# A pre-norm block with sliding-window attention and a gated feed-forward part: maxima of two query tiles turned in one pass, projection weights due sooner, second layer norms and the last gate and up products issued sooner

## The chip, the cores and the metric

The kernel runs on one core of a Trainium2 chip. The core has five engines with a queue of instructions each: TensorE (PE) multiplies matrices and transposes, VectorE (DVE) and ScalarE (ACT) work on rows and read PE's results, GpSimd (POOL) works here on rows in SBUF, and SyncE (SP) issues the transfers (DMA). The queues run beside each other and meet at semaphores. PE writes into PSUM, which the kernel uses as eight banks of 128 x 512 floats; a bank is in use from the first product written to it until the last read of it. The metric is the device time of one execution in microseconds, the median of several; lower is better.

## The reference

```python
h  = x + A(layernorm(x))          # S = 2048 tokens, D = 448
h2 = h + B(layernorm(h))

def A(x):                         # 16 heads of 28, window of 256 keys
    q, k, v = split(x @ wqkv)
    scores = q @ k.T * 28 ** -0.5
    scores = where(0 <= i - j < 256, scores, -1e9)
    return (softmax(scores) @ v) @ wo

def B(x):                         # 1792 hidden columns
    return (gelu(x @ w_gate) * (x @ w_up)) @ w_down
```

All in float32. The kernel keeps that precision by writing an operand as the sum of two rounded numbers, a "hi" part (ACT rounds it, L308) and a "lo" part, the rest (DVE or POOL subtract, L311), and by multiplying hi x hi, hi x lo and lo x hi.

## The kernel before

Nothing here is a loop of the hardware. The program is recorded as a list of operations, each with an engine, a cost, a latency, a due number called key and what it reads and writes; `Lists.run` then plays them against a model of the engines and writes each engine's queue in the order that comes out (L110 to L203): at each step, among the operations of an engine that could start soonest, the one with the lowest key goes next. A transfer is reckoned to land after a fixed time and its share of a common bus. PSUM banks are handed out by `allowed`: score products use banks 0 and 1, probability products and the passes of the maxima 2 and 3 (bank 7 joins both once all projections are done), the layer norms, v, projections and output products 6 and 7, and attention sums 4 and 5. The order is thus fixed when the program is built; on the chip the queues only wait for each other.

The tokens are 16 tiles of 128, in four chunks (c) of four tiles. The heads are four groups (g) of four, worked on in two passes (p) over the sequence. So attention has 16 blocks, B = 8p + 2c + g % 2, and a block's keys begin at 16 B.

*Before a block.* `layer_norms` computes mean and variance (DVE L338, L340; POOL L329 to L335), normalises (ACT L352), transposes on PE (L357) and writes the transposed tile xT as hi and lo. `values` multiplies v (PE L468), `project_tile` q and k (PE L502); q and k go to DRAM and return in another layout as rq and rk (SP L512, L514, L534). The weights are loaded into the staging tile raw (wqk at SP L476, two halves of 512 columns in turn; wv at L452, columns 0 to 895) and split by ACT and DVE. The second pass over the sequence needs new weights: its wv and wqk go through the same raw, wv first, and each is split into the place of the first pass's weights once these have had their last use.

*In a block.* `scores(B, i, j)` multiplies query tile i of head j with its three key tiles (PE L551, 84 rows) and takes the row maximum (DVE L555) into column j of mx. `maxima(B, i)` negates four such columns, splits them into hi and lo (DVE L570, L573) as eight columns of mhl, turns them into eight rows by one PE product against the identity (L582, 72 columns of weights, 128 columns moved), and ACT copies these eight rows into rows 96 to 103 of rq for all four heads (ACT L308, `rq<-bank`). `probs(B, m, j)` then multiplies key tile m with up to three query tiles on 104 rows (PE L622), so that the maximum is subtracted within the product, and ACT takes the exponential (L626). Key tile m meets query tiles max(0, m-2) to min(3, m). POOL cuts the diagonal blocks (L637), `attend` multiplies with v (PE L656), `drain` divides by the sums, and `output` multiplies with wo (PE L694) and adds to the residual hres (DVE L697).

*Feed-forward.* The 1792 hidden columns are 14 records of 128 (gate, up and down weights). Four groups of 4, 4, 3 and 3 records run over the four chunks, which makes 56 calls of `product`: 11 gate and 11 up products (PE L783), gelu (ACT L801), multiplication (DVE L803), rounding to hi (ACT L308) and lo (DVE L311), and 12 down products (PE L810) into four banks, which are added to hres after the last record of a group (DVE L815) and, in the last group, stored (SP L818). The keys of product n begin at 1000 + 30 n (FFN). The first two products are "early": they run in attention's last blocks and their results wait in the front part of v's tile (ACT L789). `weights` loads a record (SP L735) into raw, or into one of two parts of v's tile, and splits it; its tile is chosen by the line with q.

Second layer norms are those of h ahead of the feed-forward part. Tiles 0 to 3 run in the second pass's blocks. Tiles 4 to 15 have keys FFN + 30 t - 60; chunk c's first product has FFN + 120 c.

Of the kernel before, what the change touches and what calls it, by code (L numbers as in the profile page):

```python
# [8 lines left out]
F32 = mybir.dt.float32  # L9
# [9 lines left out]
NF = F // 128  # L19
# [19 lines left out]
FFN = 1000  # L39
EARLY = 2  # L40
# [26 lines left out]
class Lists:  # L67
# [42 lines left out]
    def run(self, allowed, idle):  # L110
# [49 lines left out]
        while n:  # L160
# [25 lines left out]
            o.fin = t + lat  # L186
# [20 lines left out]
def block_kernel(ctx: ExitStack, tc, x, wqk_in, wv_in, wo_in, ffn_in, out):  # L207
# [32 lines left out]
    mx = [pool.tile([128, 4], F32, name=f"mx{i}") for i in range(4)]  # L240
# [214 lines left out]
    def wv_split(p):  # L455
        key = 80 if p else -38
        for b in range(0, 4, 2):
            op("act", 0.47, 0.57, key, lambda b=b: to_hi(wv[:, 0, b:b + 2], wv_raw[p][:, b:b + 2]),
               [WVRAW(p, b, 2)], [WV(0, b, 2)])
            op("dve", 0.54, 0.63, key + 1, lambda b=b: to_lo(wv[:, 1, b:b + 2], wv_raw[p][:, b:b + 2], wv[:, 0, b:b + 2]),  # L460
               [WVRAW(p, b, 2), WV(0, b, 2)], [WV(1, b, 2)], port=True)
# [16 lines left out]
    def wqk_split(m):  # L478
        i = m % 4
        key = -34 + 3 * m if m < 4 else 16 * 8 - EDGE - WIN - 10 + m  # L480
        op("act", 0.53, 0.64, key, lambda: to_hi(wqk[i][:, 0], wqk_raw[m % 2]), [WQKRAW(m % 2)], [WQK(i, 0)])
        op("dve", 0.6, 0.7, key, lambda: to_lo(wqk[i][:, 1], wqk_raw[m % 2], wqk[i][:, 0]),
           [WQKRAW(m % 2), WQK(i, 0)], [WQK(i, 1)], port=True)
# [59 lines left out]
    def scores(B, i, j):  # L543
# [10 lines left out]
        def most():  # L554
            nc.vector.tensor_tensor_reduce(junk[s % 2][:, o:384], bank[b.k][:, o:384], mask[:, o:384],  # L555
                                           1.0, -BIG, OP.add, OP.max, mx[i][:, j:j + 1])
# [7 lines left out]
    def maxima(B, i):  # L564
        u, k = B % 2, (4 * B + i) % 3
        a, m = mx[i], mhl[k]
        key = 16 * B + 4 * i + LAG_T

        def hi():
            nc.vector.tensor_scalar(m[:, 0:4], a, -1.0, None, op0=OP.mult)  # L570

        def lo():
            nc.vector.scalar_tensor_tensor(m[:, 4:8], a, -1.0, f(m[:, 0:4]), op0=OP.mult, op1=OP.subtract)  # L573
        al = [("mx", i, j) for j in range(4)]
        op("dve", 0.08, 0.175, key - 2.5, hi, al, [("mh", k)], port=True)
        op("dve", 0.08, 0.17, key - 2.5, lo, al + [("mh", k)], [("ml", k)], port=True)
        b = Bank("extra")

        def tr():
            nc.tensor.matmul(bank[b.k][0:72, 384:512], m[:, 0:72], one_r,  # L582
                             start=True, stop=True)
# [142 lines left out]
    def weights(i, key):  # L726

        q = 0 if i < 2 else i % 3
# [42 lines left out]
    def product(n, i, c, k, gn, gi, down):  # L771
# [35 lines left out]
        for q in range(4):  # L807
            b = down[q]
            for a, (oh, wh) in enumerate(((0, 0), (1, 0), (0, 1))):
                op("pe", mm(D), 0.38, key + 2 * NP + 3 * q + a, lambda a=a, oh=oh, wh=wh, q=q, b=b: nc.tensor.matmul(  # L810
                    bank[b.k][:, 0:D], gh(oh)[:, q, :], get()[0][2][wh], start=(k == 0 and a == 0),
                    stop=(k == gn - 1 and a == 2)), [at[oh], *rat[2][wh]], (), b, tag="down")
# [18 lines left out]
    for p in range(2):  # L831
        for c in range(CS):
# [127 lines left out]
```

## Time and profile before

| | |
|---|---|
| median of 3 runs | 773.45 us (770.64 to 774.01) |
| the profiled execution | 775.56 us |
| its span, first to last instruction | 773.8 us |
| PE products and PE weight loads | 4280 each |
| transfers | 70.83 MB, 92 GB/s on average |

The page divides the span into 40 slices of 19.3 us:

```
PE   5999999999999999999999999999999999999996
PEld 5787788787878787768878788888888888888885
DVE  7777866676677879748432443213332322223232
ACT  6657756576666878685232331111131111111111
POOL 3413334243343457562000000000000000000000
DMA  8887547655655456215200020000000000001111
```

A digit is the busy share in tenths. The first 17 or 18 slices are layer norms, projections and attention, the rest is the feed-forward part. In the timeline a row is: start, duration, engine, line, operation, what it writes and reads, shape, count, and in brackets how long the engine stood idle ahead of it and whose work ended that. A PE product's duration runs until its last result and overlaps the next; the distance from start to start is what it takes from PE. PEld are the weight loads that run ahead of the products. In the list of waits the three numbers are the total, the times and the longest.

### The profile page before, as it was taken

To read this page: it belongs to the slowest core of one execution; us is meant where nothing else is said; L and a number is where in the kernel's file an instruction comes from. 1 tells how busy PE (TensorE), PEld (TensorE's weight loads), DVE (VectorE), ACT (ScalarE), POOL (GpSimd) and SP (SyncE) were. 2 spreads that over 40 slices of the span, in tenths; PEclk is the share of its full clock that TensorE was granted. 3 is DMA by queue.
4 is the path that set the end of the run, shared out by engine and by line. 5 is a ranking of instruction groups with operands and counts; after the bars stand their busy time and mean duration, and the time that the engine had idled before them with its cause. 6 is when DMAs were issued, how large, how long until landed. Compare 5 with 4: busy or idle time off the path is not lost.

```text
span 773.8 us, 11634 instructions
## 1 busy us (share of the span) xinstructions
PE 748.5 (97%) x4280; PEld 624.2 (81%) x4280; DVE 404.3 (52%) x1103; ACT 337.3 (44%) x735; POOL 154.8 (20%) x248
## 2 busy tenths in 40 slices
PE   5999999999999999999999999999999999999996
PEld 5787788787878787768878788888888888888885
DVE  7777866676677879748432443213332322223232
ACT  6657756576666878685232331111131111111111
POOL 3413334243343457562000000000000000000000
PEclk9999999999999999999999999999999999999999
DMA  8887547655655456215200020000000000001111
GB/s 273 248 265 214 146 123 206 175 172 132 190 166 169 131 171 171 75 54 182 78 1 0 1 82 36 0 1 0 1 1 1 0 1 1 0 1 48 48 48 47
DMA packets 44455, 70.83 MB, mean 92 GB/s; under 512 B 3854, under 2 KB 34510, under 8 KB 44366
## 3 DMA queue, kind: packets, MB, share of 16 engines
q1 hardware_dynamic: 44398, 70.09, 29.8%
q8 instruction: 33, 0.54, 0.3%
q14 instruction: 24, 0.20, 0.1%
HBM read 44.04 MB, written 25.69 MB: 90 GB/s over the span
## 4 chain that ended last, share of the span: by engine, by line
PE 85%; DMA 6%; DVE 4%; ACT 3%; issue 1%; POOL 0%; DVEq 0%; SPq 0%; ACTq 0%
PE bank L783 35%; PE bank L810 17%; PE bank L502 8%; PE bank L622 6%; PE bank L551 5%; PE bank L656 4%; PE bank L694 4%; PE bank L468 4%; DMA rk<-k 2%; PE bank L357 1%; DMA q<-proj 1%; DVE bnst L338 1%; DMA raw<-in_wqk_dram 1%; DMA raw<-in_ffn_dram 1%; ACT proj L308 1%
## 5 line engine op out<-in xcount | busy, mean ns | idle before, releaser
L555 DVE CUSTOM_DVE_ANT_0 mt<-bank,mt 128x384 bf16<-128x384 f32 (+2 forms) x256 | 128.7, 526 | 47.0 <-PE bank L551 45.7
L626 ACT ACTIVATE pp<-bank 128x384 f32<-128x384 f32 (+2 forms) x352 | 126.1, 388 | 60.0 <-PE bank L622 52.1
L803 DVE TENSOR_TENSOR mt<-bank,mt 128x512 f32<-128x512 f32 x54 | 37.4, 692 | 208.9 <-PE bank L783 208.9
L502 PE MATMUL bank<-xT,proj 128*128 128x512 f32 x308 | 104.0, 409 | 0.9 <-DVE hres L697 0.8
L637 POOL TENSOR_SCALAR_AFFINE_SELECT pp<-pp 128x512 f32<-128x512 f32 x120 | 74.6, 635 | 125.4 <-ACT pp L626 124.1
L622 PE MATMUL bank<-rq,rk 104*128 104x384 f32 (+2 forms) x352 | 99.1, 302 | 0.2
L801 ACT ACTIVATE mt<-bank 128x512 f32<-128x512 f32 x54 | 32.4, 599 | 149.5 <-PE bank L783 149.5
L308 ACT ACTIVATE proj<-mt 128x512 fp32r<-128x512 f32 x56 | 35.3, 630 | 142.3 <-DVE mt L803 142.3
L783 PE MATMUL bank<-xT,proj 128*128 128x512 f32 x352 | 93.0, 393 | 0.0
L783 PE MATMUL bank<-xT,rec 128*128 128x512 f32 x352 | 91.0, 395 | 0.0
L783 PE MATMUL bank<-xT,rk 128*128 128x512 f32 x352 | 90.9, 393 | 0.0
L551 PE MATMUL bank<-rk,rq 84*128 84x384 f32 (+2 forms) x256 | 82.4, 346 | 2.3 <-DMA rk<-k 1.5
L622 PEld LDWEIGHTS bank<-rq,rk 104*128 104x128 f32 x352 | 65.3, 190 | 15.6 <-ACT pp L626 3.8
L783 PEld LDWEIGHTS bank<-xT,rec 128*128 128x128 f32 x352 | 66.1, 188 | 13.6
L783 PEld LDWEIGHTS bank<-xT,rk 128*128 128x128 f32 x352 | 65.9, 188 | 12.6
L783 PEld LDWEIGHTS bank<-xT,proj 128*128 128x128 f32 x352 | 65.8, 188 | 11.7
L502 PEld LDWEIGHTS bank<-xT,proj 128*128 128x128 f32 x308 | 56.7, 192 | 8.3 <-issue 1.4
L468 PE MATMUL bank<-proj,xT 128*128 128x224 f32 x352 | 59.9, 280 | 1.2 <-DVE proj L311 0.6
L468 PEld LDWEIGHTS bank<-proj,xT 128*128 128x128 f32 x352 | 52.6, 192 | 3.5 <-DVE proj L311 1.1
L551 PEld LDWEIGHTS bank<-rk,rq 84*128 84x128 f32 x256 | 47.1, 190 | 10.1 <-DVE mx L555 3.6
L311 DVE TENSOR_TENSOR proj<-mt,proj 128x512 fp32r<-128x512 f32 x56 | 39.1, 698 | 30.0 <-ACT proj L308 29.2
L810 PE MATMUL bank<-rk,proj 128*128 128x448 f32 x192 | 47.8, 369 | 2.7 <-ACT proj L308 2.7
(90 smaller groups left out, 1019.7 us busy)
## 6 DMA issues: line engine op xcount, KB each, us to landing
rk<-k SPq DMA_DIRECT2D x44, 336.0 KB
rq<-q SPq DMA_DIRECT2D x32, 336.0 KB
q<-proj SPq DMA_DIRECT2D x16, 448.0 KB
v<-in_ffn_dram SPq DMA_DIRECT2D x8, 736.0 KB
k<-proj SPq DMA_DIRECT2D x12, 448.0 KB
raw<-in_ffn_dram SPq DMA_DIRECT2D x6, 736.0 KB
hres<-in_x_dram SPq DMA_DIRECT2D x16, 224.0 KB
q<-proj SPq DMA_DIRECT2D x16, 224.0 KB
```

Of the source, the lines that this page charges most:

```text
L308: nc.scalar.activation(dst, src, AF.Copy)
L311: (eng or nc.vector).tensor_sub(dst, src, f(hi))
L468: op("pe", mm(224), 0.29, key + a / 16, lambda a=a, h=h, wb=wb, xb=xb: nc.tensor.matmul(bank[b.k][:, 0:224], xT[:, xb, t * 128:(t + 1) * 1 ...
L502: op("pe", mm(512) + 0.002, 0.403, key, lambda a=a, h=h, wb=wb, xb=xb: nc.tensor.matmul(bank[b.k], wqk[i][:, h, wb, :], xT[:, xb, c * 512: ...
L551: nc.tensor.matmul(bank[b.k][:, o:384], rq[u][0:3 * DH, j, i * 128:i * 128 + 128], rk[u][0:3 * DH, j, m0 * 128:(i + 3) * 128], start=True, ...
L555: nc.vector.tensor_tensor_reduce(junk[s % 2][:, o:384], bank[b.k][:, o:384], mask[:, o:384], 1.0, -BIG, OP.add, OP.max, mx[i][:, j:j + 1])
L622: nc.tensor.matmul(bank[b.k][:, 0:n], rk[u][0:104, j, m * 128:m * 128 + 128], rq[u][0:104, j, lo * 128:(hi + 1) * 128], start=True, stop=True)
L626: nc.scalar.activation(pp[:, j, o * 128:o * 128 + n], bank[b.k][:, 0:n], AF.Exp, scale=SCALE)
L637: nc.gpsimd.affine_select(a, a, pattern=[[0, 4], [-cm, 128]], compare_op=op_, fill=0.0, base=0, channel_multiplier=cm)
L783: op("pe", mm(512), 0.403, key + q * NP + a / NP, lambda a=a, h=h, wb=wb, xb=xb, q=q, b=b: nc.tensor.matmul(bank[b.k], get()[0][q][h][:, w ...
L803: op("dve", 0.605, 0.702, key + 2 * NP, lambda: nc.vector.tensor_tensor(blocks(ge), src(1), blocks(ge), op=OP.mult), ["ge", *held[1]], ["g ...
L810: op("pe", mm(D), 0.38, key + 2 * NP + 3 * q + a, lambda a=a, oh=oh, wh=wh, q=q, b=b: nc.tensor.matmul(bank[b.k][:, 0:D], gh(oh)[:, q, :], ...
```

## The change

Maxima of two tiles. `mx` becomes two tiles of two times four columns; `maxima(B, h)` is called after query tiles 1 and 3 and handles tiles 2h and 2h + 1. The second tile's eight columns stand 32 columns behind the first's in `mhl`, so that one pass gives the first tile's rows on partitions 0 to 7 and the second's on 32 to 39, and ACT copies each with an instruction of its own. The key is that of the pair's second tile.

```diff
-    mx = [pool.tile([128, 4], F32, name=f"mx{i}") for i in range(4)]
+    mx = [pool.tile([128, 2, 4], F32, name=f"mx{i}") for i in range(2)]
...
-    def maxima(B, i):
-        u, k = B % 2, (4 * B + i) % 3
-        a, m = mx[i], mhl[k]
-        key = 16 * B + 4 * i + LAG_T
+    def maxima(B, h):
+        u, k = B % 2, (2 * B + h) % 3
+        a, m = mx[h], mhl[k][:, 0:64].rearrange("p (i n) -> p i n", i=2)
+        key = 16 * B + 8 * h + 4 + LAG_T
...
-            nc.tensor.matmul(bank[b.k][0:72, 384:512], m[:, 0:72], one_r,
-                             start=True, stop=True)
-
-        def put():
-            to_hi(rq[u][96:104, :, i * 128:i * 128 + 128],
-                  bank[b.k][0:8, None, 384:512].to_broadcast([8, 4, 128]))
+            nc.tensor.matmul(bank[b.k][0:72, 384:512], mhl[k][:, 0:72], one_r, start=True, stop=True)
+
+        def put(i):
+            t = 2 * h + i
+            to_hi(rq[u][96:104, :, t * 128:t * 128 + 128],
+                  bank[b.k][32 * i:32 * i + 8, None, 384:512].to_broadcast([8, 4, 128]))
         op("pe", mm(128), 0.24, key, tr, [("mh", k), ("ml", k), "one"], (), b)
-        op("act", 0.55, 0.6, key, put, (), [("rx", u, i)], b)
+        for i in range(2):
+            op("act", 0.55, 0.6, key, lambda i=i: put(i), (), [("rx", u, 2 * h + i)], b)
...
-                    maxima(B, i)
+                    if i % 2:
+                        maxima(B, i // 2)
```

Second pass's weights: lower keys for the loads and splits of wv and wqk, and a planner that reckons each transfer after 15 us to land 0.8 later.

```diff
+MARGIN = 0.8
...
-            o.fin = t + lat
+            o.fin = t + lat + (MARGIN if e == "sp" and t > 15 else 0)
...
-        key = 80 if p else -38
+        key = 66 if p else -38
...
-        key = -34 + 3 * m if m < 4 else 16 * 8 - EDGE - WIN - 10 + m
+        key = -34 + 3 * m if m < 4 else 72 + m
...
-            wv_load(1, 84)
+            wv_load(1, 62)
...
-                wqk_load(m, 16 * 8 - EDGE - WIN - 16 + m)
+                wqk_load(m, 66 + m)
```

(EDGE is 9 and WIN 14, so the old keys of wqk are 89 + m for the load and 95 + m for the split.) Feed-forward: the third record goes through raw in place of a part of v's tile; second layer norms from tile 4 on have keys lower by 50; and the down products of the last but one product have keys higher by 30, behind the last product's gate and up products.

```diff
+LEAD = 110
...
-        q = 0 if i < 2 else i % 3
+        q = 0 if i < 3 else i % 3
...
-                op("pe", mm(D), 0.38, key + 2 * NP + 3 * q + a, lambda a=a, oh=oh, wh=wh, q=q, b=b: nc.tensor.matmul(
+
+                late = 30 if n == 4 * NF - 2 else 0
+                op("pe", mm(D), 0.38, key + late + 2 * NP + 3 * q + a, lambda a=a, oh=oh, wh=wh, q=q, b=b: nc.tensor.matmul(
...
-                                if t < 4 else FFN + 30 * t - 60, "ln2")
+                                if t < 4 else FFN + 30 * t - LEAD, "ln2")
```

All other keys stand as they were, but the planner plays the whole list anew, so the order of other instructions moves too.

More of the change, by code (lines that the diff above doesn't have):

```diff
@@ L555, in most @@
             nc.vector.tensor_tensor_reduce(junk[s % 2][:, o:384], bank[b.k][:, o:384], mask[:, o:384],
-                                           1.0, -BIG, OP.add, OP.max, mx[i][:, j:j + 1])
+                                           1.0, -BIG, OP.add, OP.max, mx[i // 2][:, i % 2, j:j + 1])
         op("pe", mm(384 - o), 0.19 + (384 - o) / 2400, s, one,
@@ L561, in scores @@
            [("mx", i, j)], b, tag="most")
-    def maxima(B, i):
-        u, k = B % 2, (4 * B + i) % 3
-        a, m = mx[i], mhl[k]
-        key = 16 * B + 4 * i + LAG_T
+    def maxima(B, h):
+        u, k = B % 2, (2 * B + h) % 3
+        a, m = mx[h], mhl[k][:, 0:64].rearrange("p (i n) -> p i n", i=2)
+        key = 16 * B + 8 * h + 4 + LAG_T
         def hi():
-            nc.vector.tensor_scalar(m[:, 0:4], a, -1.0, None, op0=OP.mult)
+            nc.vector.tensor_scalar(m[:, :, 0:4], a, -1.0, None, op0=OP.mult)
         def lo():
-            nc.vector.scalar_tensor_tensor(m[:, 4:8], a, -1.0, f(m[:, 0:4]), op0=OP.mult, op1=OP.subtract)
-        al = [("mx", i, j) for j in range(4)]
+            nc.vector.scalar_tensor_tensor(m[:, :, 4:8], a, -1.0, f(m[:, :, 0:4]), op0=OP.mult, op1=OP.subtract)
+        al = [("mx", i, j) for i in (2 * h, 2 * h + 1) for j in range(4)]
         op("dve", 0.08, 0.175, key - 2.5, hi, al, [("mh", k)], port=True)
```

## The prediction

> **What bounds the kernel now.** I read the page first, then the busy time by stretches, the list of waits, and the timeline at each place where TensorE (PE) stood still.
>
> ```profile
> span 773.8 us, 11634 instructions
> ...
> PE 748.5 (97%) x4280; PEld 624.2 (81%) x4280; DVE 404.3 (52%) x1103; ACT 337.3 (44%) x735; POOL 154.8 (20%) x248
> ...
> PE 85%; DMA 6%; DVE 4%; ACT 3%; issue 1%; POOL 0%; DVEq 0%; SPq 0%; ACTq 0%
> ```
>
> PE is busy for 97% of the span and holds 85% of the chain that ended last. So an edit pays if it takes a slot from PE or closes a gap of PE; it costs if PE has to stand where it did not before. By stage:
>
> ```profile
> 60.00:340.00 280.00, 274.77 (x2031) 222.63 (x2030) 205.84 (x715) 195.98 (x495) 123.69 (x176) 0.99 0.54 156
> 340.00:404.00 64.00, 60.46 (x304) 50.39 (x303) 37.36 (x68) 29.98 (x53) 11.58 (x18) 1.00 0.24 84
> 404.00:760.00 356.00, 355.21 (x1614) 300.32 (x1613) 110.90 (x175) 71.50 (x118) 0.00 (x0) 1.00 0.04 15
> ```
>
> The columns after the length are busy PE, PE's weight loads, DVE, ACT, POOL, then the granted clock and DMA. Attention (60 to 340) leaves PE 5.2 us idle of 280, the passage into the feed-forward part (340 to 404) 3.5 of 64, the steady feed-forward part 0.8 of 356. That last stage can't be shortened by order alone; everything below is won ahead of 440 or in the last 12 us.
>
> **Maxima of two query tiles in one pass.** 64 passes become 32, with the same 72 columns of weights.
>
> ```profile
> L582 PE MATMUL bank<-one,mhl 128*72 128x128 f32 x64 | 14.7, 229 | 1.0 <-ACT rq L308 0.9
> ```
>
> ```profile
> 329.79 0.14 PEld L582 LDWEIGHTS bank<-one,mhl 128*72 128x72 f32 x1
> 329.91 0.22 PE L582 MATMUL bank<-one,mhl 128*72 128x128 f32 x1
> 329.91 0.54 PEld L783 LDWEIGHTS bank<-xT,proj 128*128 128x128 f32 x3
> 329.97 0.92 PE L783 MATMUL bank<-xT,proj 128*128 128x512 f32 x3
> ```
>
> The 229 ns are one pass from end to end, and mostly overlap its neighbours. What a pass takes from PE is the distance to the next start: 0.06 us in the matmuls (329.91 to 329.97), 0.12 us in the weight loads (329.79 to 329.91). With PE bound by the one or the other this is 32 x 0.06 = 1.9 us to 32 x 0.12 = 3.8 us; among the short products of attention the loads are nearly as dense as the matmuls (222.6 against 274.8 us), so I take the middle, **2.9 us gained**. The Trainium skill ("TensorE: Matmul & The Clock Gate", LDWEIGHTS (loading the stationary operand)) gives a load as columns / 1.2 ns, for 72 columns 60 ns; by that the saving is an estimated 1.9 us and the sum below 7.2, while the load slot in the trace is twice as long.
>
> DVE loses 64 small instructions, and ACT keeps its 64 copies into rq:
>
> ```profile
> L570 DVE TENSOR_SCALAR mhl<-mx x64: 123/170/1206, 42.0 to 326.5; 128x4 fp32r<-128x4 f32 x64
> ...
> L308 ACT ACTIVATE rq<-bank x64: 585/586/592, 42.9 to 330.7; 8x512 fp32r<-8x512 f32 x64
> ```
>
> 64 x 0.17 = 10.9 us less DVE, which isn't on the path (206 of 280 us busy): nothing. The bank of a pass is held through two copies (2 x 0.59) in place of one, but half as often: nothing.
>
> The price is lateness. Tile 0 now waits for the maxima of tile 1, tile 2 for those of tile 3, and the probabilities of key tile 2 need query tile 2.
>
> ```profile
> 136.71 0.22 PE L582 MATMUL bank<-one,mhl 128*72 128x128 f32 x1
> ...
> 136.97 0.58 ACT L308 ACTIVATE rq<-bank 8x512 fp32r<-8x512 f32 x1 [0.24 <-PE bank L582]
> ```
>
> From the start of a pass to its first row in rq is 136.71 to 137.55 = 0.84 us with ACT free, 1.43 us to the second. In the built orders I counted the PE work between a pass and the first probability product that needs it, in start-to-start slots: for tiles 2 and 3 it was 1.1 to 7.8 us, and for the second pair it is now 0.9 to 2.6 us in all 16 blocks. An exponential ahead in ACT's queue is enough to make PE stand; behind that product in PE's queue stand scores and projections that were ready. Such waits exist already:
>
> ```profile
> PEld bank L622 <- ACT rq L308: 2.2, 6, 0.6
> ```
>
> ```profile
> 74.67 0.28 PE L582 MATMUL bank<-one,mhl 128*72 128x128 f32 x1 [0.91 <-ACT rq L308]
> ```
>
> Six waits cost 2.2 us, mean 0.37, longest 0.6. With 8 or 9 of them it is 3.2, so I take **1.0 us lost**; the bounds are 2.2 gained (none left) and 16 x 0.6 - 2.2 = 7.4 lost. The second row is a pass that waited for a bank behind a copy; with half the passes I take back half of the 1.0 us that PE idled before L582 (its group's row above): **0.5 gained**, bounds 0 and 1.0.
>
> **Projection weights.** The one large hole of attention is here:
>
> ```profile
> 140.48 0.83 SPq L476 DMA_DIRECT2D raw<-in_wqk_dram  x2
> ...
> 146.77 0.63 ACT L308 ACTIVATE proj<-raw 128x512 fp32r<-128x512 f32 x1 [3.50 <-DMA raw<-in_wqk_dram]
> ...
> 148.65 0.45 PE L551 MATMUL bank<-rk,rq 84*128 84x384 f32 x1 [0.74 <-DVE mx L555]
> ...
> 149.88 0.72 PE L502 MATMUL bank<-xT,proj 128*128 128x512 f32 x2 [0.78 <-DVE hres L697]
> ```
>
> ```profile
> 140.00:150.00 10.00, 8.48 (x61) 6.50 (x60) 6.27 (x20) 5.20 (x13) 1.27 (x2) 1.00 0.71 178
> 150.00:154.00 4.00, 4.00 (x13) 3.33 (x14) 3.76 (x14) 1.50 (x3) 1.36 (x3) 0.57 0.65 218
> ```
>
> The load takes 6.3 us, ACT stands for it 3.5, DVE behind ACT, and PE twice, 1.5 us together. Then the clock is granted at 0.57 for 4 us, which loses 4 x 0.43 = 1.7 us. The new keys (66 + m for 89 + m) don't load sooner in the built order: the weights for v are split only when the first half's last v tile is through PE, and the loads of wqk need the raw that this split frees. On SP they still stand behind the same pair of rq and rk loads, on ACT the first split behind as many exponentials (112). What does move is DVE: the residual add that freed the bank for the product at 149.88, and one more score's maximum, now stand ahead of the split's low half. So at best both stands go and with them the low clock, 3.2 us; at worst nothing. I take half, **1.6 us gained**. The Trainium skill ("TensorE: Matmul & The Clock Gate", Part 1: The HAM clock gate) lets the clock fall only after an idle window of about 3.4 us; by that the low clock didn't come from these stands, 0.8 would be my half and the sum 7.4. The row speaks against it: the clock fell with 1.5 us idle in ten.
>
> The margin of 0.8 us on planned landings reorders all of attention a little. Three waits of PE for rk cost 1.5 us in the list of waits; I count nothing, with 1.5 to either side.
>
> **Second layer norms and the passage.**
>
> ```profile
> 400.29 0.62 ACT L308 ACTIVATE proj<-mt 128x512 fp32r<-128x512 f32 x1
> ...
> 400.96 0.70 PEld L810 LDWEIGHTS bank<-rk,proj 128*128 128x128 f32 x4 [1.01 <-ACT proj L308]
> 400.96 2.39 PE L810 MATMUL bank<-rk,proj 128*128 128x448 f32 x9 [0.77 <-ACT proj L308]
> ```
>
> ```profile
> 434.02 2.39 PE L810 MATMUL bank<-rk,proj 128*128 128x448 f32 x9 [0.77 <-ACT proj L308]
> ```
>
> Two layer-norm tiles are transposed at once just ahead of a down product, and ACT evacuates the first of them before it rounds the hidden block. In the new order one tile stands between a product's last down and the next gate, so gate work covers it: 2 x 0.77 = **1.5 us gained**; no instruction is added. The same form at 368.57 has a second cause:
>
> ```profile
> 365.30 1.62 ACT L308 ACTIVATE rec<-v 128x512 fp32r<-128x512 f32 x3 [1.25 <-DMA v<-in_ffn_dram]
> ...
> 368.57 0.87 PE L810 MATMUL bank<-rk,proj 128*128 128x448 f32 x3 [1.16 <-ACT proj L308]
> ```
>
> ACT was late from a weight record too, and still splits three records between two hidden blocks. Of 1.16 I take half, **0.6**. Into the third product:
>
> ```profile
> 342.10 0.62 ACT L308 ACTIVATE rk<-raw 128x512 fp32r<-128x512 f32 x1
> 342.62 0.62 ACT L308 ACTIVATE rq<-v 128x512 fp32r<-128x512 f32 x1
> ...
> 343.29 4.38 PE L783 MATMUL bank<-xT,rq 128*128 128x512 f32 x18 [1.59 <-ACT rq L308]
> ```
>
> The third record now goes through raw, and its split stands right behind the first gelu: an evacuation of xT and a split of rk no longer precede it (1.2 us), one evacuation of an early product does (0.6). **0.6 us gained**, bounds 0 and 1.59.
>
> **Last product.**
>
> ```profile
> 762.55 2.73 PE L783 MATMUL bank<-xT,rec 128*128 128x512 f32 x11
> 765.38 0.69 DVE L803 TENSOR_TENSOR mt<-bank,mt 128x512 f32<-128x512 f32 x1 [5.49 <-PE bank L783]
> 766.11 0.63 ACT L308 ACTIVATE proj<-mt 128x512 fp32r<-128x512 f32 x1 [3.37 <-DVE mt L803]
> ...
> 766.79 2.70 PE L810 MATMUL bank<-rec,proj 128*128 128x448 f32 x12 [1.51 <-ACT proj L308]
> ```
>
> PE stands 1.51 us for multiply and rounding. The twelve downs of the product before, 2.70 us as these twelve show, now stand in that gap: **1.5 us gained**. Late next are the last four residual adds and their store, as now.
>
> **Sum.** 2.9 - 1.0 + 0.5 + 1.6 + 1.5 + 0.6 + 0.6 + 1.5 = 8.2 us. Against the profiled execution (775.56 us, 1.8 of it outside the span) this is 767.4. That execution is 2.1 above the median of the runs shown, 773.45; for the median I forecast **765.2 us**.
>
> **Rivals.** *Late maxima* (slower): PE stands at all 32 passes' first users. The other terms bring 9.2; with 32 waits it breaks even at (9.2 + 2.2) / 32 = 0.36 us each; at the longest wait seen, 0.6, it costs 17.0 and the time is 781.2. For it: the shrunken distance. Against it: first pairs keep 3.0 us or more. 5%.
> *Attention gives it back*: score, maximum, copy and exponential form a ring over few banks, and ACT and DVE are 70 to 74% busy there; then only the passage and the tail count, 4.2 us, 769.2. 17%.
> *The weights' edit does nothing*, as its place on SP says: 766.8, within the forecast's own spread and counted there.
> *Shared raw*: the fourth record's load now waits until POOL has made the third's low parts.
>
> ```profile
> 343.31 1.30 POOL L311 TENSOR_TENSOR rq<-v,rq 128x512 fp32r<-128x512 f32 x1 [3.30 <-ACT rq L308]
> ...
> 346.03 2.86 POOL L311 TENSOR_TENSOR rq<-v,rq 128x512 fp32r<-128x512 f32 x2
> ...
> 354.05 5.12 PE L810 MATMUL bank<-proj 128*128 128x448 f32 x24
> ```
>
> ```profile
> 351.11 6.16 DMA raw<-in_ffn_dram
> ```
>
> From 348.9, plus 6.2 us as that load took in the chain, plus 1.6 for three splits on ACT (as at 365.30), is 356.7; PE begins the fourth product after these downs, near 359.2, 2.5 us later. A record 5.5 us later than this reckoning, its load taking nearly twice as long, makes PE stand 3: 768.2. 8%.
> *Everything lands*: no late copies, the whole hole at 146 to 154, 1.16 and 1.59 whole: 8.2 + 1.0 + 1.6 + 0.6 + 1.0 = 12.4, 761.0. 15%. Forecast: 55%.
>
> **How the numbers follow.** The range is 760.5 to 770.5: it takes in everything lands, shared raw and most of attention gives it back, and leaves out the slower case and about an eighth beside it. Half a per cent (3.9 us) is what a measurement tells from no change; the bounds are 769.6 and 777.3. Faster: forecast, everything lands, most of shared raw and half of the giving back, 0.82; within, 0.13; slower, 0.05.
>
> **What would show it.** 32 passes and PE's instructions down by 32; no wait of a down for ACT near 401 and 434; PE without a break from the last gate to the last down; the first wqk split still waiting 3 us for its load, with or without a clock below 0.9 behind it; waits of L622's successor for rq below 4 us. It is wrong if those waits pass 8 us, if a new wait for a record stands ahead of the fourth product, or if attention is no shorter though it has 32 passes less.

## The result, and the profile after

| | before | changed |
|---|---|---|
| median of four runs each, side by side | 772.05 us (770.54 to 774.01) | 759.34 us (758.88 to 760.09) |
| ratio, 95% interval | | 0.9835 (0.9805 to 0.9865) |
| span of the profiled execution | 773.8; of a second one 769.9 | 757.5 |
| PE products | 4280 | 4248 |

The kernel is 12.7 us faster: 5.9 below the forecast of 765.2, and 1.2 below the lower end of its range. The forecast started from 773.45, the median of the first three runs, and side by side the kernel before had 772.05: 1.4 of the 5.9 is this baseline, 4.5 the sum of 8.2. The page of the changed kernel, with busy times and the chain that ended last:

```profile
span 757.5 us, 11508 instructions
...
PE 740.9 (98%) x4248; PEld 620.8 (82%) x4248; DVE 393.7 (52%) x1039; ACT 334.5 (44%) x735; POOL 155.5 (21%) x248
...
PE 89%; DVE 4%; ACT 2%; DMA 1%; issue 1%; POOL 1%; SPq 0%; ACTq 0%; DVEq 0%
```

The kernel before was profiled once more (e7 below). That execution's span is 3.9 us shorter than the first one's; its clock is granted at 1.00, as the changed kernel's is, and it is the one to compare with. Its chain reads:

```profile
PE 89%; DVE 4%; DMA 3%; ACT 2%; issue 1%; POOL 0%; DVEq 0%; SPq 0%; ACTq 0%
```

So PE holds as much of the chain as before, and DMA goes from 3 to 1%. Busy time by stretches, first the second execution of the kernel before, then the changed kernel:

```profile
60.00:340.00 280.00, 274.00 (x2053) 221.70 (x2051) 206.97 (x716) 198.07 (x498) 123.47 (x176) 1.00 0.53 155
340.00:404.00 64.00, 62.11 (x293) 52.73 (x294) 36.71 (x67) 27.50 (x50) 11.58 (x17) 1.00 0.25 83
```

```profile
60.00:340.00 280.00, 277.38 (x2056) 224.78 (x2055) 204.99 (x673) 204.36 (x515) 132.03 (x186) 1.00 0.53 156
340.00:404.00 64.00, 63.44 (x300) 54.17 (x299) 33.58 (x63) 24.87 (x44) 5.68 (x9) 1.00 0.24 84
```

PE idles 2.6 us of 280 in place of 6.0, and 0.6 of 64 in place of 1.9. Where the time came from is read by setting the same gate or up product side by side in both traces: the first that isn't early starts at 340.23 before and 333.86 after (6.4 us won in attention), the 353rd at 460.68 and 450.54 (3.8 more in the passage), the 1211th at 753.63 and 743.54 (no change in 290 us), and the spans end at 769.92 and 757.50 (2.3 more in the last product). Between the first two of these products the kernel before has 40 transposes and the changed one 32; the other eight, 0.7 us by the distances below, stand ahead of them, in attention. Counted for the same work, attention won 7.1 and the passage 3.1. The sum of 8.2 had 4.6, 2.1 and 1.5 for these three places: every one of them brought more. One execution against another isn't exact: e4 below has every instruction up to the last product in the same order as the changed kernel, and its trace reaches the first of these products at 335.46, 1.6 later.

The passage: a chunk's start in the kernel before (second execution), then in the changed one.

```profile
395.59 1.03 PE L357 MATMUL bank<-ident,xn 128*128 128x128 f32 x8
397.39 2.39 PE L810 MATMUL bank<-rk,proj 128*128 128x448 f32 x9 [0.77 <-ACT proj L308]
399.62 0.39 PE L783 MATMUL bank<-xT,proj 128*128 128x512 f32 x1
```

```profile
385.47 0.77 PE L814 MATMUL bank<-rq,proj 128*128 128x448 f32 x3
386.08 0.60 PE L359 MATMUL bank<-ident,xn 128*128 128x128 f32 x4
386.43 2.77 PE L785 MATMUL bank<-xT,rk 128*128 128x512 f32 x11
389.04 1.98 PE L785 MATMUL bank<-xT,proj 128*128 128x512 f32 x8
```

The bracket says that the wait cost 0.77. From start to start it cost more. Four transposes with work right behind them take 0.35 (386.08 to 386.43), so eight take 0.70; before, the eight took 1.80 (395.59 to 397.39), 1.10 too many. Three downs take 0.61 (385.47 to 386.08), so nine take 1.83; behind the wait they took 2.23, 0.40 too many. That is 1.5 us for this chunk start. (At the first of the three, near 365, the same reckoning gives 1.91 for the transposes and so 1.2.) The bracket counts idle time only from the modelled end of the last transpose, which lies inside the stand, and it doesn't count that the downs behind it come at wider distances.

The last product in the changed kernel:

```profile
748.69 1.99 PE L814 MATMUL bank<-rk,proj 128*128 128x448 f32 x9
748.96 0.69 DVE L805 TENSOR_TENSOR mt<-bank,mt 128x512 f32<-128x512 f32 x1 [3.07 <-PE bank L785]
749.68 0.64 ACT L310 ACTIVATE proj<-mt 128x512 fp32r<-128x512 f32 x1 [2.77 <-DVE mt L805]
...
750.52 0.78 PE L814 MATMUL bank<-rec,proj 128*128 128x448 f32 x3
...
751.95 1.69 DVE L819 TENSOR_TENSOR hres<-bank,hres 128x448 f32<-128x448 f32 x3 [0.90 <-PE bank L814]
...
753.80 0.62 DVE L819 TENSOR_TENSOR hres<-bank,hres 128x448 f32<-128x448 f32 x1 [0.16 <-PE bank L814]
```

The nine downs fill the time of multiply and rounding; PE's next start follows at 750.52, 1.83 behind the first of them, which is their own time, so nothing is left of the stand. And the four banks now end one after the other, so that three of the last four residual adds are done before PE's last product ends, where all four ran at the end before.

In attention, the place of the weights, the waits of PE for maxima and the passes:

```profile
142.91 0.62 DVE L699 TENSOR_TENSOR hres<-bank,hres 128x448 f32<-128x448 f32 x1 [0.66 <-PE bank L696]
...
143.42 0.63 ACT L310 ACTIVATE proj<-raw 128x512 fp32r<-128x512 f32 x1 [2.94 <-DMA raw<-in_wqk_dram]
...
144.08 0.69 DVE L313 TENSOR_TENSOR proj<-raw,proj 128x512 fp32r<-128x512 f32 x1
...
147.58 0.44 PE L553 MATMUL bank<-rk,rq 84*128 84x384 f32 x1 [0.15 <-DVE mx L557]
```

```profile
PEld bank L624 <- ACT rq L310: 1.0, 3, 0.6
```

```profile
L583 PE MATMUL bank<-one,mhl 128*72 128x128 f32 x32 | 7.5, 234 | 0.0
```

ACT still waits 2.94 us for the load, so the weights don't come sooner; but the residual add (142.91) stands ahead of the split's low half (144.08), and PE idles 0.15 where it stood twice. The waits for maxima didn't grow with the shorter distance: 1.0 us in 3 places, after 2.2 in 6. PE stands ahead of no pass for a bank. There are two new waits, for ACT and POOL, in the 24 output products from 339.78 on: they take 6.05 from start to start, where they took 4.86 before.

### The profile page after: what moved, and what is told of

Read it like the earlier page. It is cut to its first block, busy times and chain, and to the rows that moved or that the text cites. A ratio compares the mean times of both kernels' runs of the same rounds, so it can differ in the third digit from the quotient of the medians.

```text
span 757.5 us, 11508 instructions
## 1 busy us (share of the span) xinstructions
PE 740.9 (98%) x4248; PEld 620.8 (82%) x4248; DVE 393.7 (52%) x1039; ACT 334.5 (44%) x735; POOL 155.5 (21%) x248
## 4 chain that ended last, share of the span: by engine, by line
PE 89%; DVE 4%; ACT 2%; DMA 1%; issue 1%; POOL 1%; SPq 0%; ACTq 0%; DVEq 0%
PE bank L785 36%; PE bank L814 18%; PE bank L504 8%; PE bank L624 6%; PE bank L553 5%; PE bank L658 5%; PE bank L470 5%; PE bank L696 4%; PE bank L359 1%; DMA raw<-in_wqk_dram 1%; DVE mt L557 1%; DVE bnst L340 1%; DMA k<-proj 1%; DVE proj L313 1%; DVE xT L313 1%
## 5 line engine op out<-in xcount | busy, mean ns | idle before, releaser
L628 ACT ACTIVATE pp<-bank 128x384 f32<-128x384 f32 (+2 forms) x352 | 122.4, 390 | 58.0 <-PE bank L624 50.9
L504 PE MATMUL bank<-xT,proj 128*128 128x512 f32 x308 | 99.9, 401 | 0.3 <-DVE xT L313 0.3
L624 PE MATMUL bank<-rq,rk 104*128 104x384 f32 (+2 forms) x352 | 95.7, 304 | 0.6 <-ACT pp L628 0.4
L785 PE MATMUL bank<-xT,proj 128*128 128x512 f32 x352 | 93.0, 393 | 0.0
L696 PE MATMUL bank<-wos,ohl 128*128 128x448 f32 x192 | 49.5, 375 | 0.6 <-POOL ohl L313 0.3
```

The lines of the kernel that those rows point to most:

```text
L504: op("pe", mm(512) + 0.002, 0.403, key, lambda a=a, h=h, wb=wb, xb=xb: nc.tensor.matmul(bank[b.k], wqk[i][:, h, wb, :], xT[:, xb, c * 512: ...
L624: nc.tensor.matmul(bank[b.k][:, 0:n], rk[u][0:104, j, m * 128:m * 128 + 128], rq[u][0:104, j, lo * 128:(hi + 1) * 128], start=True, stop=True)
L628: nc.scalar.activation(pp[:, j, o * 128:o * 128 + n], bank[b.k][:, 0:n], AF.Exp, scale=SCALE)
L696: op("pe", mm(D), 0.38, wk, lambda a=a, h=h, oh=oh, wh=wh, i=i, k=k: nc.tensor.matmul(bank[k.k][:, 0:D], ohl[:, h, oh, i * 128:(i + 1) * 1 ...
L785: op("pe", mm(512), 0.403, key + q * NP + a / NP, lambda a=a, h=h, wb=wb, xb=xb, q=q, b=b: nc.tensor.matmul(bank[b.k], get()[0][q][h][:, w ...
```

## The experiments

Differences are of medians, against 759.34 where the changed kernel is edited and against the kernel before of the same comparison where that one is; ratios are against the kernel before. Beside e13 to e16 that kernel had 774.35, since five of its nine executions there show a mean granted clock of 0.997 or 0.998; the other four have a median of 771.6, near its usual 772, so medians are compared there too (e7 has more on the clock).

**How much each part holds, taken out of the changed kernel.** e1 issues every pass four times, 96 passes more. e2 goes back to one pass a tile. e3 sets LEAD to 60, e4 late to 0, e5 MARGIN to 0, and e6 sends the third record through v again.

```diff
# e1
+            for _ in range(4):
-            nc.tensor.matmul(bank[b.k][0:72, 384:512], mhl[k][:, 0:72], one_r, start=True, stop=True)
+                nc.tensor.matmul(bank[b.k][0:72, 384:512], mhl[k][:, 0:72], one_r, start=True, stop=True)
# e2, with mx, mhl and maxima as in the kernel before
-                    if i % 2:
-                        maxima(B, i // 2)
+                    maxima(B, i)
# e3
-LEAD = 110
+LEAD = 60
# e4
-                late = 30 if n == 4 * NF - 2 else 0
+                late = 0
# e5
-MARGIN = 0.8
+MARGIN = 0.0
# e6
-        q = 0 if i < 3 else i % 3
+        q = 0 if i < 2 else i % 3
```

> The changed kernel with each of its 32 passes of the maxima issued four times into the same bank (96 passes more, the same order of everything else). Slot theory (a pass takes from PE only its start-to-start slot, 0.06 to 0.12 us): 96 x 0.06 to 0.12 = 5.8 to 11.5 us longer than the changed kernel, at the 0.09 of the prediction 8.6, about 768. Rival (a pass is dear in itself, 0.2 us or more from PE): 19 us or more longer, above 778.

Measured 762.93, ratio 0.9879 (0.9861 to 0.9898): 3.6 slower, less than the 5.8 to 11.5 expected, 0.037 us for each added pass. In the trace each added pass takes 0.060 of PE's starts; more than a third of that doesn't show in the time. So 32 passes less are worth 1.2 to 1.9 us by themselves. Standing single among other products, as in both kernels, a pass takes 0.060 to its next start too, in the median. These distances sum to 5.8 us before (e7) and 3.1 after, but in each kernel two of them hold a stand of the next product, one of 0.90 for a bank among them; without these, 62 passes take 4.3 and 30 take 2.1, 2.2 less.

> The changed kernel with the maxima of one tile at a time again (64 passes), all other edits kept. Slot theory as in the prediction's sum (2.9 and 0.5 gained, 1.0 lost to lateness): 2.4 us longer than the changed kernel, about 761.7. Rival (each pass is a meeting of DVE, PE, ACT and a bank, so that half the meetings save more than their slots, and nothing is lost to lateness): 5 to 7 us longer, 764 to 766.

Measured 763.53, ratio 0.9889 (0.9869 to 0.9908): 4.2 slower, between the 2.4 of the sum and the 5 to 7 of the rival.

> The changed kernel with the second layer norms' keys as before (FFN + 30 t - 60), all other edits kept. By the prediction's terms the two waits near the chunk starts return, and perhaps the one at 368: 1.5 to 2.1 us longer, 760.8 to 761.4. Rival (the whole passage from 340 to 436 us was bought by the layer norms, 4.3 us between the two traces): about 763.5.

Measured 765.19, ratio 0.9912 (0.9894 to 0.9931): 5.8 slower, more than either expectation. The wait is back with the very numbers of the kernel before:

```profile
391.19 1.03 PE L359 MATMUL bank<-ident,xn 128*128 128x128 f32 x8
393.00 2.39 PE L814 MATMUL bank<-rk,proj 128*128 128x448 f32 x9 [0.77 <-ACT proj L310]
395.22 0.39 PE L785 MATMUL bank<-xT,proj 128*128 128x512 f32 x1
```

1.81 for eight transposes and 2.22 for nine downs, 1.5 us lost again. Against the changed kernel's trace, this one is 2.0 late by the fifth product, 3.9 by the tenth and 5.8 by the fifteenth: 1.9 for each of these two chunk starts. Of each 1.9, 0.35 are four transposes that the changed kernel has behind it by the fifth product and this one doesn't, which leaves 1.5, the same as within the trace. The 2.0 ahead of them are another matter: the 24 output products take 8.48 from start to start in this run, with waits for ACT and DVE, after 6.05 in the changed kernel and 4.86 in the kernel before. So 2.4 of the 5.8 are lost at a place where the kernel before loses nothing, and e3 overstates what the keys were worth.

> The changed kernel with the down products of the last but one product ahead of the last gate and up products again, all other edits kept; only PE's order differs, in its last rows. The prediction's term: 1.5 us longer, 760.8. Rival (the last residual adds are shortened as well, 2.3 us between the two traces): 761.7.

Measured 761.96, ratio 0.9860 (0.9839 to 0.9882): 2.6 slower, not 1.5. The stand is back:

```profile
750.23 2.74 PE L785 MATMUL bank<-xT,rec 128*128 128x512 f32 x11
754.48 2.73 PE L814 MATMUL bank<-rec,proj 128*128 128x448 f32 x12 [1.51 <-ACT proj L310]
```

Eleven such products take 2.61 where nothing waits (386.43 to 389.04 above), and here the next start comes 4.25 later: 1.6 lost where the bracket says 1.51. Most of the rest is the four residual adds, all behind the last product again: from the 1211th product to the end of the span it is 2.3 more than in the changed kernel.

> The changed kernel with the planner's margin of 0.8 us on transfers set to 0, all other edits kept. Theory (the margin keeps PE off the holes behind late transfers, the one at the second pass's projection weights above all): the hole returns, with or without the low clock, 1.5 to 3.2 us longer than the changed kernel, 760.8 to 762.5. Rival (pairing the maxima alone moved the residual add and the scores ahead of the split, the margin adds nothing): within 0.7 us of 759.3.

Measured 764.35 (761.97 to 767.94), ratio 0.9890 (0.9865 to 0.9915): 5.0 slower, more than the 1.5 to 3.2 expected. Two waits of PE for keys are in its timeline that the changed kernel doesn't have:

```profile
156.91 0.58 PE L553 MATMUL bank<-rk,rq 84*128 84x384 f32 x2 [0.82 <-DMA rk<-k]
...
274.13 0.59 PE L553 MATMUL bank<-rk,rq 84*128 84x384 f32 x2 [1.20 <-DMA rk<-k]
```

They make 2.0 of the 5.0. At the weights one of the two stands is back, 0.72 us for a score's maximum; the residual add still comes ahead of the split. The waits for maxima are 3.3 us in 7 places.

> The changed kernel with the third record loaded into a part of v's tile again, all other edits kept. The prediction's term: 0.6 us longer, 759.9. Rival (the passage needs the early products' results out of their banks, and these can go to v's tile only after the record has been split): 1.6 us or more, 761 or above.

Measured 760.96, ratio 0.9842 (0.9818 to 0.9866): 1.6 slower. In its trace the stand at the entry into the feed-forward part is 2.63 from start to start, after 0.89 in the changed kernel. Three of its four executions show a clock of 0.997 or 0.998; the one at 0.999 took 759.33, no more than the changed kernel. So what the late record costs may be the low clock behind the stand (the last section shows it) as much as the stand.

**The kernel before, and the parts put into it alone.** e7 is the kernel before unchanged. e8 adds the pairs alone, e9 the margin alone, and e12 the three edits of the feed-forward part (LEAD 110, the third record through raw, late).

> The kernel before, unchanged, profiled once more. Theory (the profiled execution of before was one of its slow ones: the clock fell to half behind the hole at 146 to 150 us in that one and not in those of 770.5): this profile shows either the half clock and a time of 773.5 or more, or no half clock and a time near 770.5. Rival (the half clock is there whatever the time): half clock with a time below 771.5, or none with one above 773.

Measured 772.09 (770.58 to 775.78), ratio 0.9994. Around the hole of the weights, the first profiled execution and then this one, with stretches cut at the low clock:

```profile
149.00:150.45 1.45, 0.67 (x4) 0.48 (x4) 1.45 (x5) 0.47 (x2) 0.00 (x0) 1.00 0.88 237
150.45:153.86 3.41, 3.41 (x11) 2.85 (x10) 3.31 (x12) 1.50 (x3) 1.22 (x3) 0.50 0.64 207
```

```profile
148.09 0.44 PE L551 MATMUL bank<-rk,rq 84*128 84x384 f32 x1 [0.80 <-DVE mx L555]
149.40 0.70 PE L502 MATMUL bank<-xT,proj 128*128 128x512 f32 x2 [0.87 <-DVE hres L697]
...
150.45:153.86 3.41, 3.41 (x21) 2.71 (x19) 3.02 (x11) 2.91 (x7) 2.06 (x3) 1.00 0.59 180
```

The same two stands are there, as long as in the first, and the clock stays at 1.00: 21 products start in the 3.41 us in place of 11. So the low clock doesn't come with these stands each time. It isn't rare either: of the 54 executions of the kernel before that stand beside the experiments, 25 have a mean clock of 0.998 or less, median 774.35, and 29 have 0.999 or 1.0, median 771.96. Where in the span it falls, only a trace shows. The changed kernel has 0.999 or 1.0 in all four executions, so against its 759.34 the gain at a full clock is 12.6. The part of the prediction's 3.2 us that came from the low clock (1.7) is not in that gain, and the first profiled execution, 2.1 us above the median, was long for the most part for that reason.

> The kernel before with the maxima of two tiles in one pass and nothing else of the change. Slot theory (2.9 + 0.5 - 1.0): 2.4 us shorter than before, 769.7. Rival (as in e2_no_pair, where taking the pairs away cost 4.2): 767.9. Third (without the margin, the later first rows make PE stand): 772 or above.

Measured 769.26, ratio 0.9951 (0.9932 to 0.9971): 3.1 faster, where the prediction's three terms for the pairs sum to 2.4. The waits for maxima are 2.4 us in 6 places, after 2.2 in 6, and no pass waits for a bank: the pairs alone lose next to nothing to lateness, and they don't win the 1.2 that the changed kernel shows. At the weights:

```profile
145.36 0.62 DVE L696 TENSOR_TENSOR hres<-bank,hres 128x448 f32<-128x448 f32 x1 [0.66 <-PE bank L693]
...
147.33 0.69 DVE L311 TENSOR_TENSOR proj<-raw,proj 128x512 fp32r<-128x512 f32 x1 [1.35 <-ACT proj L308]
...
149.58 0.45 PE L551 MATMUL bank<-rk,rq 84*128 84x384 f32 x1 [1.35 <-DVE mx L555]
```

The residual add (145.36) stands ahead of the split's low half (147.33) here too, with the old keys and no margin, and the stand that it ended in the kernel before is gone. The other stand, for a maximum, is longer (1.35 after 0.80 in e7).

> The kernel before with the planner's margin of 0.8 us on transfers and nothing else of the change. Theory (the margin keeps PE off the holes behind late transfers whatever the rest of the order): 2 to 5 us shorter than before, 767 to 770, with the stands near 148 us and behind rk gone from the timeline. Rival (the margin only happened to give a good order together with the other edits): within 1 us of 772.

Measured 772.05 (769.56 to 772.83), ratio 0.9983 (0.9972 to 0.9995): 0.9 faster. At the weights PE doesn't stand any more, since the first load is issued 9.5 us sooner than in the prediction's rows (140.48) and ACT finds it landed:

```profile
131.03 0.85 SPq L476 DMA_DIRECT2D raw<-in_wqk_dram  x2
135.30 0.63 ACT L308 ACTIVATE proj<-raw 128x512 fp32r<-128x512 f32 x1
```

Its trace is some 3 us ahead of e7's through the second half of attention, and loses this at one place:

```profile
334.13 1.50 PE L656 MATMUL bank<-pp,v 128*29 128x384 f32 x24
338.43 4.93 PE L783 MATMUL bank<-xT,rq 128*128 128x512 f32 x14 [2.80 <-ACT rq L308]
```

```profile
336.26 1.08 ACT L308 ACTIVATE rk<-raw 128x512 fp32r<-128x512 f32 x2
337.24 0.62 ACT L308 ACTIVATE proj<-mt 128x512 fp32r<-128x512 f32 x1
337.76 1.60 ACT L308 ACTIVATE rq<-v 128x512 fp32r<-128x512 f32 x3
```

PE comes out of attention sooner and waits for the third record, whose split stands on ACT behind two splits of the one before and a rounding; in this execution a window of low clock follows as well. The stand, from start to start, is 1.2 longer than in e7; most of the rest of the 3 us is the low clock. Seven of the twelve executions have a clock of 0.998 or less; the other five have a median of 771.00.

> The kernel before with the three edits of the feed-forward part (earlier second layer norms, third record through raw, last gate and up products first) and nothing else. By the prediction's terms 4.2 us shorter than before, 767.9. Theory from the traces (PE loses 1.4 us, not 0.8 to 1.2, at each of the three waits behind a pair of layer norms, and 2.3 at the end): 6 us shorter, 766.1.

Measured 765.58, ratio 0.9902 (0.9886 to 0.9918): 7.4 faster than the kernel before beside it, 6.5 against its usual 772.05. Predicted for these edits were 4.2. By the spans of two profiled executions at a clock of 1.00, this one and e7, it is 6.0: 3.6 up to the 1211th product and 2.3 in the last. None of its five executions has a clock under 0.999, though the two stands at the weights are as in the kernel before.

**What the margin is.** e11, e13, e10 and e14 set it to 0.4, 1.2, 1.6 and 2.4 in the changed kernel.

```diff
-MARGIN = 0.8
+MARGIN = 0.4   # e11; 1.2 in e13, 1.6 in e10, 2.4 in e14
```

> The changed kernel with a margin of 0.4 us. Theory (a cover against late transfers): between the two that were measured, 759.3 at 0.8 and 764.4 at 0. Rival (another draw): below 759 or above 765, or no longer than at 0.8.

> The changed kernel with a margin of 1.6 us in place of 0.8. Theory (a margin is a cover against late transfers, and 0.8 is nearly enough): 758 to 760.5, no wait of PE for rk. Rival (each margin just draws another order, good or bad): 761 or above.

> The changed kernel with a margin of 1.2 in place of 0.8. Theory draw: the margin is no cover that a larger one improves; each value draws another order of attention, and what it brings is the waits that this order happens to have. Then 1.2 lands anywhere between 759 and 765, like 0, 0.4, 0.8 and 1.6 (764.4, 765.2, 759.3, 761.0). Rival cover: transfers land about 0.8 later than the planner reckons, and any margin from 0.8 on keeps PE from waiting for them; then 1.2 is 759 to 761 and no wait of PE for rk of 0.6 us or more is left in its trace.

> The changed kernel with a margin of 2.4. Theory draw: between 759 and 765. Rival cover: 759 to 761, and no wait of PE for rk of 0.6 us or more. If 1.2 and 2.4 both lie at 759 to 761, four values from 0.8 on agree and the two below lie 4 us higher, which speaks for cover.

| margin | 0 | 0.4 | 0.8 | 1.2 | 1.6 | 2.4 |
|---|---|---|---|---|---|---|
| median, us | 764.35 | 765.24 | 759.34 | 761.40 | 761.00 | 766.99 |
| ratio to before | 0.9890 | 0.9895 | 0.9835 | 0.9839 | 0.9847 | 0.9914 |
| PE waits for rk in the list, us | 2.0 | 1.3 | none | none | none | none |

Neither theory holds by itself. The margin does cover late landings: from 0.8 on, PE's products wait for no rk any more in these four traces, and the two values below are 5 us slower or more by the medians (3.3 to 3.6 by the two executions of each that have a clock of 1.0). But the largest covers too and is the slowest of all. It has these in place of the waits for rk (list of waits, 2.4):

```profile
PEld bank L624 <- ACT pp L628: 7.1, 21, 0.9
PEld bank L624 <- ACT rq L310: 3.7, 8, 0.7
```

In the changed kernel these are 3.8 in 11 and 1.0 in 3. Yet at 1.2 they are 6.1 in 15 and 3.8 in 10, at 1.6 5.8 in 17 and 3.5 in 10, and those two kernels are 6 us faster, so these waits don't explain 2.4. Its trace is 4.2 us behind the changed kernel's at the first product that isn't early and 3.3 more at the 353rd, where output products wait 2.2 us; a window of low clock at 309 us is part of the 4.2. So 1.3 to 2.0 us of what a margin of 0.8 brings are waits for keys, shown. That the rest is which order of attention the planner happens to find is argued and not shown; 0.8 is the best of the six that were run.

**Are the parts worth more together?** e15 puts the margin and the third record through raw into the kernel before.

```diff
+MARGIN = 0.8
...
-            o.fin = t + lat
+            o.fin = t + lat + (MARGIN if e == "sp" and t > 15 else 0)
...
-        q = 0 if i < 2 else i % 3
+        q = 0 if i < 3 else i % 3
```

> The kernel before with two parts of the change alone: the margin of 0.8 and the third record through raw. The margin alone brought 1, but its trace had PE stand 2.86 us for the third record's split at the entry into the feed-forward part (1.65 in the kernel before, 0.89 in the changed one). Theory: attention gained more than 1 and the late record took it back, so the two together bring 3 to 4: 768 to 769.5. Rival: margin and record add up as they did singly (1 and 1.6 at most): 769.5 to 771.

Measured 768.08 (766.52 to 769.88), ratio 0.9928 (0.9904 to 0.9953), where the margin alone has 0.9983: 4 us more by the ratios (0.0055 of 772), though the record is worth 1.6 in the changed kernel. The entry in its timeline, to be set against 2.80 in e9:

```profile
335.69 1.50 PE L656 MATMUL bank<-pp,v 128*29 128x384 f32 x24
338.02 4.19 PE L783 MATMUL bank<-xT,rq 128*128 128x512 f32 x17 [0.83 <-ACT rq L308]
```

So the late record took back a good part of what attention gained, as the theory had it: of the 4 us some 2 are in this stand. None of its six executions has a clock under 0.999, where e9 has seven of twelve, which is some of the rest.

**A try at more.** e16 sets LEAD to 140.

> The changed kernel with second layer norms issued sooner still, LEAD 140 in place of 110. The waits for the hidden block are gone at 110 (0.6 us of lost starts between 360 and 440 are left), so nothing is left to gain there: 758.5 to 760.5. It would be slower, 761 to 764, if the layer norms of tiles 4 to 7 now fall into attention's last block, where ACT and DVE are busy.

Measured 761.17 (760.68 to 762.26), ratio 0.9838 (0.9806 to 0.9870): nothing gained. Its trace is 0.4 ahead up to 285 us, then loses 1.5 within some 20 us, where PE waits for exponentials on ACT and this execution has a window of low clock. All four executions have a clock of 0.995 to 0.998, so what LEAD 140 gives without that isn't known. No version that was run beats the changed kernel.

## Why the prediction was wrong in size

Its direction, and the places where the gain would arise, were right. Each term, by the second execution of the kernel before and the changed one (starts lost are the distance to the next start beyond the usual one of the same product):

| term of the sum | predicted | shown |
|---|---|---|
| 32 passes less | 2.9 | 2.2, distances to the next start where nothing waits |
| lateness of the maxima | -1.0 | +1.2, waits for rq 2.2 before, 1.0 after; -0.2 with the pairs alone (e8) |
| bank waits of the passes | 0.5 | 0.9, all of it |
| hole of the weights | 1.6 | 1.7, starts lost 2.0 before, 0.3 after |
| margin | 0 | 0.7, waits for rk 0.7 before, none after |
| third record, entry | 0.6 | 0.8, starts lost 1.65 and 0.89 |
| layer norms and 368.57 | 1.5 + 0.6 | 3.1, by the same product in both traces and for the same transposes |
| last product | 1.5 | 2.3 to 2.6 |

The terms as shown sum to 12.9 and more. The first score starts 1.2 later in the changed profile (40.69 after 39.53), in the part ahead of attention, which leaves 11.7; the spans differ by 12.4. The other 0.7 us wasn't traced to a place; three of the terms are differences of waits from the list, and such a wait falls short of what it costs.

*The step that failed first is the price of a stand.* "2 x 0.77 = 1.5" and "of 1.16 I take half" took the brackets for the cost. Three chunk starts cost 1.2 to 1.5 each from start to start, 4.2 together where the sum had 2.1, and the first of them, counted by half, went whole. e3 brings two of them back at 1.5 each, and e12 shows a like size without any change in attention. The sum also left out what it cost: the output products behind the third product lose 1.2 in the changed kernel, so 3.1 remain. The term of the last product has the same fault (1.51 for 1.6) and left out that the residual adds would also end sooner, which it called "as now"; e4 measured 2.6.

*The second is the loss for lateness*, the largest single miss at 2.2 us. With the pairs alone, PE's waits for rq are 2.4 us after 2.2 (e8), so 0.9 to 2.6 us of work behind a pass, against 0.84 to the first row, was nearly enough. That they fall to 1.0 comes with the margin of 0.8, and not with a margin as such: in the changed kernel they are 3.3 at a margin of 0, 1.2 at 0.4, and 3.5 to 3.8 from 1.2 on, more than the 3.2 that the prediction reckoned. The order that came out at 0.8 was a lucky one. The bounds (2.2 gained, 7.4 lost) held the value, and the choice within them was on the wrong side. The rival of late maxima fell with it. The price of a pass missed the other way: 0.09 was taken, the middle of 0.06 and 0.12, and 0.06 was right.

*Weights.* "At best both stands go" is what happened to the stands, by the mechanism that the prediction gave: the residual add, and a maximum, ahead of the split's low half. That the size agrees is luck: 1.6 was half of the stands and of the low clock, and the stands went whole, while the low clock isn't in the comparison. That the keys do nothing is borne out by the built orders: with the old keys in the changed kernel, every engine's instructions stand in the same order. What moved DVE's instructions was the pairs for the residual add (e8 has it without the margin, and so has e5), and the margin for the maximum: the stand for it is 1.35 in e8, 0.72 in e5 and 0.15 in the changed kernel. The prediction put both under the weights' edit. The Trainium skill's rule that it weighed ("TensorE: Matmul & The Clock Gate", Part 1: The HAM clock gate) would have had the low clock not come from these stands. e7 shows the stands without it, so they alone don't bring it; but the last section has eight windows with PE never idle throughout the time ahead, so the rule, read as a window without any work, isn't borne out either.

*The margin* was left at 0 with 1.5 to either side. Alone it is worth 0.9, in the changed kernel 5.0 (3.6 by the two executions of e5 at a clock of 1.0). This is the widest miss among the bounds. e9 and e15 show one reason: it is worth what the stages behind it let through.

*The rivals.* Nothing of "attention gives it back" or "shared raw" is in the trace: no wait for a record stands ahead of the fourth product. "Everything lands", 761.0 at 15%, came nearest; its gain of 12.4 is almost the 12.7 measured. That is luck in part: it counted 1.7 of low clock that isn't in the comparison, and priced the stands by their brackets.

## What to carry to other kernels

A stand's price is the distance between starts on both sides of it, less what the same instructions take where nothing waits, with the thinned queue behind it counted in; the idle time in brackets is a lower bound, half of the price at the chunk starts here. In a kernel whose order a planner makes, edits of order aren't worth a fixed sum each: what one stage gains waits at the next stage's late item, so price them together, and give each its effect with the late item and without it. Profile the kernel before twice and look at the clock of every run, since a chance event in the only execution can end up as a term of the sum. When distances are summed, take out those that hold a wait which another term counts, and count the same work on both sides.

## What was not expected of the hardware

The granted clock falls to 0.50 for one window of 3.41 us in some executions and not in others of the same program. Of the 18 profiles of this case, seven have such a window ahead of the end, one of them two, each behind some idle time of PE. But the stands don't decide it: the kernel before has a clock of 0.50 behind stands of 0.74 and 0.78, and none behind stands of 0.80 and 0.87 at the same place in another execution. e6, one more, at its entry:

```profile
330.00:338.00 8.00, 5.43 (x49) 3.89 (x47) 4.61 (x8) 7.74 (x17) 3.51 (x7) 1.00 0.22 85
338.00:341.40 3.40, 3.40 (x9) 2.64 (x8) 2.37 (x5) 3.22 (x6) 3.40 (x3) 0.50 0.24 54
```

In the 3.41 us ahead of these windows PE idled between 0.3 and 2.5 us, never throughout; stretches as long with 1.6 to 2.1 us idle elsewhere had none behind them. The length agrees with the window of 3413 ns that the Trainium skill gives ("TensorE: Matmul & The Clock Gate", Part 1: The HAM clock gate), and that it runs free, as the same section says, would let the same stand fall into one window or be split over two. Which idle share decides was not tried.
